# Summing two bit patterns of VectorE's exponential by an accumulating transfer instead of GpSimd, with new order constants

## The chip, the cores and the metric

The kernel runs on one core of a Trainium2 chip. The core's engines run side by side and meet only at semaphores: TensorE (PE in the profile) multiplies matrices into PSUM, ScalarE (ACT) evaluates functions, VectorE (DVE) and GpSimd (POOL) do elementwise work, SyncE (SP) and the queues of the other engines issue DMA transfers. The metric is the device time of one execution in microseconds (us), lower is better.

## The reference

With x of 2048 rows by 448 columns (bf16), the kernel computes `x + s * g`. Both s and g start from the layer-normalised rows xn:

- s is self-attention with 16 heads of 28 columns: `qkv = xn @ wqkv`, scores `q k^T * 28^-0.5`, softmax over the 2048 keys, times v, then `@ wo`.
- g is `silu(gelu(xn @ w1 + b1) @ w2 + b2)` with 1792 hidden columns.

The part that matters here is the softmax: 16 x 2048 x 2048 exponentials, 67 million of them.

## The kernel before, in words

**Tiles.** The scores are made transposed: 128 keys by 512 queries of one head make one score tile, one PSUM bank. Four heads form a head group, four groups of 512 queries a chunk list, so there are 16 blocks (a head group and a query chunk, order `ORD`, line 29) of 64 tiles each (16 key tiles of 4 heads), 1024 tiles in all. A tile goes through three steps: a score matmul (line 1431, K = 28 rows padded to 32, so four heads can share the array by rows), an exponential, and a product with v (the PV matmul, line 1867, four heads side by side in the array's columns) which adds into one PSUM bank `acc`. A column of v holds a constant, so the sum of the exponentials comes out of the same matmul. At the end of a block VectorE copies `acc` away (line 1930), and a chain of small transfers, a reciprocal (line 1949 on GpSimd, or line 1947 on VectorE) and a multiplication (line 1958, GpSimd) normalises it.

**Two ways to an exponential.** Most tiles go to ScalarE, two or three at a time: one ACTIVATE reads two or three PSUM banks (1024 or 1536 columns) and writes bf16 (`fexp`, line 1487). The others are taken in groups of four (the four heads of one key tile) by VectorE. A group's four tiles are read from PSUM, one at a time, by a tensor_scalar that scales and shifts them and writes uint16 (`p_apass`, line 1716): these integers, read as bf16, are a coarse exponential. Two more passes over all four tiles (2048 columns, SBUF to SBUF) add a constant to the integers (`p_expq`, line 1775; constants 40 and 82 of `SH`), which gives three bit patterns of one exponential. Their weighted sum, first pattern times 1 and the other two times `VC` = 0.6875, is the better exponential. The sum is not formed: the PV matmul runs over all three, with v for the first and a copy of v scaled by VC (`vs`, made at line 1800) for the others. So such a group takes 12 PV matmuls instead of 4.

**Summing the two patterns ahead.** The second and third pattern have the same weight, so they may be added beforehand. Then the group needs 8 PV matmuls, and one of its three buffers comes free early. `p_expq` does that on GpSimd where the constants say so (`MG` on, at least `GE` tiles before the block's end, and GpSimd free within `GQ` us): four additions of 128 x 512 (line 1788).

**Buffers.** The patterns live in `unit` buffers of 128 x 2048 bf16, made of space that other tensors no longer use (x_sb, w2, wq, wk, kT, h, xnT, vaug, qsq). There are up to 23 of them, many only late in the kernel. A group begins only when three are free.

**The order.** The instruction order of every engine is fixed when the program is built: a list scheduler in the kernel file (`run`, `start_of`, `put`) walks through time with a duration and a latency for every task and puts the task that can start first. Constants steer it: `BP` has a row for each block of 64 tiles (`p_scores` changes rows), with the pace, the look-ahead and the priorities for that block; `NQ` says how many times per block a VectorE group may be asked for. Which tiles VectorE takes is a result of this walk, so the constants decide how many groups there are. On the chip every engine executes its list in order; a task waits on a semaphore until what it reads is there.

**Other work** fills the gaps between score matmuls: the projections to q, k and v, the two layers of the MLP (lines 1279 and 1348), with one uninterrupted stage where ScalarE evaluates gelu, and at the end the output projection (line 1968). Two thirds down the kernel four output transfers are issued from GpSimd with `accum_op=ALU.add`, onto an output that already holds x (line 1994).

Of the kernel before, what the change touches and what calls it, by code (L numbers as in the profile page):

```python
# [8 lines left out]
ALU = mybir.AluOpType  # L9
ET = mybir.EngineType  # L10

PE, ACT, DVE, POOL, SP = ET.PE, ET.Activation, ET.DVE, ET.Pool, ET.SP
# [16 lines left out]
ORD = [(b // C, b % C) for b in range(11)] + [(3, 0), (3, 1), (3, 2), (2, 3), (3, 3)]  # L29

GM = 584
BPN = ('MG', 'GQ', 'GE', 'EPS', 'PV0', 'PVC', 'MP', 'ND4', 'LU', 'JOINT', 'LQ', 'JMAX', 'DQ', 'URG', 'SLACK', 'UR', 'QLEAD', 'QDIST', 'R3', 'OP')
BP = (
# [17 lines left out]
)  # L51
NQ = (5, 11, 13, 13, 12, 7, 11, 10, 16, 3, 16, 15, 12, 15, 9, 14)
QLEAD, QDIST = 0, 12
JMAX, DQ, LQ, ND4, LU = 2, 3, 2, 3, 3
PV0, PVC, MP = 12, 4, 0.3
SLACK = 0.3
# [4 lines left out]
MG, GQ, GE = 1, 4.0, 12  # L61
GP, MP4, GL = 4.64, 1, 1.2
URG = 12
# [21 lines left out]
    n += k  # L85
SBT = [(f // FT, f % FT) for f in range(F0)]
SEM, OWN = 0.07, 0.03
SWITCH = 0.1
JOINT = 0.05
EPS = 0.1  # L90
# [20 lines left out]


class _Task:
    __slots__ = ("E", "fn", "reads", "writes", "dur", "lat", "rank", "w", "mode", "rows", "port")

    @property
    def prio(self):
# [2 lines left out]
    def __init__(self, E, fn, reads=(), writes=(), dur=0.1, lat=0.05, prio=5, w=1.0, mode="full", rows=(), port=False):  # L120
        self.E, self.fn, self.reads, self.writes = E, fn, list(reads), list(writes)
        self.dur, self.lat, self.rank, self.w = dur, lat, prio, w
        self.mode, self.rows, self.port = mode, set(rows), port
        if E == DVE:
            ov = min(OVERLAP, 0.4 * self.dur)
            self.dur, self.lat = self.dur - ov, self.lat + ov


class _Kernel:
# [74 lines left out]
    def put(self, t, start=None):  # L204
        if start is None:
            start = self.start_of(t)
        self.deps(t.E, t.reads, t.writes)
        if t.E == POOL and t.port:
            self.wait(POOL, self.dve_port)
        sem = self.evsem[t.E]  # L210
        self.evcnt[t.E] += 1
        if t.E == DVE and t.port:
            self.dve_port = (sem, self.evcnt[t.E])
        self.prog[t.E].append(lambda eng, f=t.fn, s=sem: f(eng).then_inc(s, 1))
        h = (sem, self.evcnt[t.E])
        if t.E == PE:
            if t.mode == self.pe_mode == "row" and not (t.rows & self.pe_rows):
                self.pe_rows |= t.rows
            else:
                self.pe_rows = set(t.rows)  # L220
            sw = SWITCH if t.mode != self.pe_mode else 0.0
            self.pe_mode, self.pe_start = t.mode, start
            self.pe_hist.append((start - sw, start + t.dur * t.w))
        if t.port:
            self.port[DVE if t.E == POOL else POOL] = start + t.dur
        self.tE[t.E] = max(self.tE[t.E], start + t.dur)
        self.mark(h, t.reads, t.writes, start + t.dur + t.lat)
        self.log.append((start, t))
        return h
# [158 lines left out]
    def alloc(self):  # L388
# [138 lines left out]
        self.s_qn = [[self.sem("s_qn%d_%d" % (q, c)) for c in range(C)] for q in range(G)]  # L527
        self.s_x0b, self.s_wqk1 = self.sem("s_x0b"), self.sem("s_wqk1")
        self.s_out = [self.sem("s_out%d" % q) for q in range(14)]
        self.s_w = {n: self.sem("s_" + n) for n in ("wqk", "wv", "w1", "w2", "wo", "b")}  # L530

    def schedule(self):
# [911 lines left out]
    def p_scores(self):  # L1444
        K = self
        u = 0
        while K.next_m < MTOT:
            yield ("until", lambda: K.exp_u >= u - 2)
            if K.next_m >= MTOT:
                break  # L1450
            if K.gu is not None and u == K.gu + 1:
                yield ("until", lambda: K.dir_read == ND)
            if K.next_m // 64 != K.blk:
                K.blk = K.next_m // 64
                K.tune(K.blk)
            b0 = 4 * (u % 2)
            n = 2
            ms = []
            while len(ms) < n and K.next_m < MTOT:
                ms.append(K.next_m)  # L1460
                K.step()
            if K.gu is None and ms[-1] >= GM:
                K.gu = u
            at = {m: K.ring[:, b0 + k, :] for k, m in enumerate(ms)}
            toks = [K.b_ring[b0 + k] for k in range(len(ms))]
            K.pend = p = {"task": K.t_score(ms, at, toks, 1), "ms": ms, "at": at, "toks": toks, "rs": [], "b0": b0}
            yield p["task"]
            K.pend = None
            for (m0, u0, m), x in p["rs"]:
                K.spawn(K.p_apass(u0, m0, m - m0, *x), m0)  # L1470
            K.sc_u = u
            u += 1
# [286 lines left out]
    def p_expq(self, m0, u):  # L1759
# [13 lines left out]
        for i in (1, 2):  # L1773
            W, T, bW = *K.pair(us[i], u), K.b_U[us[i]]
            yield _Task(DVE, lambda eng, W=W, T=T, i=i: eng.tensor_scalar(W.bitcast(u16), T.bitcast(u16), float(SH[i]), None, op0=ALU.add),  # L1775
                        bT, bW, 0.69, 0.0, 4, port=True)
        K.ln2e = 0
        if MG and K.next_m < 64 * (m0 // 64 + 1) - GE and K.tE[POOL] < K.now + GQ:
            v, w = us[1:]
            for k in range(0, 4, MP4):  # L1780
# [10 lines left out]
            K.late_ready.append((m0, ((u, 0), (v, 1))))  # L1791
            return
        K.late_ready.append((m0, ((us[0], 0), (us[1], 1), (us[2], 1))))

    def p_vs(self, g):
        K = self
# [275 lines left out]
```

## Time and profile before

| what | value |
|---|---|
| time, median of 3 runs | 419.19 us (419.13 to 419.26) |
| span of the profiled execution, first to last instruction | 417.0 us |
| outside the span, median minus span | 2.2 us |
| granted TensorE clock, mean | 0.999 |
| ScalarE: exponentials of 2 tiles / of 3 tiles | 283 / 74 |
| VectorE: passes from PSUM (line 1716) / integer additions (line 1775) | 236 / 118 |
| GpSimd: additions of two patterns (line 1788) | 52 |
| GpSimd: accumulating output transfers (line 1994) | 4 |

The profile has no time of its own beside its span; the median of the unprofiled runs lies 2.2 us above the span, and this difference is taken as fixed.

How to read it: each page line of a group names the source line, the engine, the operation, what it writes and reads, the shape and the count; behind the first bar the busy time in us and the mean of one in ns; behind the second the engine's idle time just before, and what ended it. Consecutive instructions of ScalarE overlap at their ends, so the distance from start to start, which the timeline gives, says what one costs; its "duration" is longer. The same holds for TensorE's matmuls.

### The profile page before, as it was taken

The page shows a single profiled execution, that of the slowest core. Times are in us where ns is not written, and L with a number is a line of the kernel's source. Part 1 is how long each engine was busy: PE and PEld are TensorE (multiplying, and loading weights), DVE is VectorE, ACT ScalarE, POOL GpSimd, SP SyncE. Part 2 cuts the span into 40 slices and gives each one's busy share as a digit, 9 for nine tenths or more (in the row PEclk, how much of TensorE's full clock was granted, in tenths as well). Part 3 has the DMA queues.
Part 4 walks back from the last instruction along what each step waited for, and adds up shares of the span by engine and source line. Part 5 has one row for each costly group of instructions (what it writes and reads, how often), then busy time and mean ns, then how long its engine had stood idle before and what let it go on. Part 6 is the DMA issues. An engine that isn't in the chain of part 4 may idle for free.

```text
span 417.0 us, 9616 instructions
## 1 busy us (share of the span) xinstructions
PE 400.2 (96%) x3651; PEld 132.6 (32%) x3651; DVE 343.3 (82%) x592; ACT 405.9 (97%) x413; POOL 183.3 (44%) x197
## 2 busy tenths in 40 slices
PE   5899999999999999999999999999999999999995
PEld 4443223332222222222223443222222222333352
DVE  8968899997786899999895115799999888989487
ACT  6999999999999999999999999999999999999995
POOL 7571333237769280204331424408421755680850
PEclk9999999999999999999999999999999999999999
DMA  8801000000001000000240100000010002202061
GB/s 265 271 2 40 3 3 26 14 17 15 26 2 28 0 2 30 2 27 3 54 130 27 25 3 2 2 2 6 21 28 3 10 20 23 50 15 59 4 146 60
DMA packets 15952, 15.29 MB, mean 37 GB/s; under 512 B 7129, under 2 KB 12993, under 8 KB 15874
## 3 DMA queue, kind: packets, MB, share of 16 engines
q1 hardware_dynamic: 15042, 13.07, 11.1%
q0 software_dynamic: 576, 0.92, 1.6%
q8 instruction: 29, 0.48, 0.5%
q10 hardware_dynamic: 288, 0.69, 0.4%
q14 instruction: 17, 0.14, 0.1%
HBM read 12.59 MB, written 2.93 MB: 37 GB/s over the span
## 4 chain that ended last, share of the span: by engine, by line
PE 72%; ACT 15%; DVE 7%; issue 5%; DMA 1%; ACTq 0%; DVEq 0%
PE ring L1431 23%; PE acc L1867 16%; PE ring L1279 9%; ACT P L1487 8%; PE ring L1348 7%; PE misc L1348 4%; PE ring L924 3%; ACT h L1487 3%; PE misc L924 3%; ACT xnT L1487 2%; PE misc L1279 2%; PE misc L1218 2%; PE ring L1218 1%; PE misc L1968 1%; ACT h L1327 1%
## 5 line engine op out<-in xcount | busy, mean ns | idle before, releaser
L1487 ACT ACTIVATE P<-ring 128x1024 bf16<-128x1024 f32 (+1 forms) x237 | 252.9, 1172 | 1.4 <-PE acc L1867 0.5
L1431 PE MATMUL ring<-qT,kT 32*128 32x512 bf16 (+2 forms) x1064 | 142.0, 358 | 6.9 <-ACT P L1487 1.5
L1487 ACT ACTIVATE h<-ring 128x1024 bf16<-128x1024 f32 (+1 forms) x80 | 87.2, 1191 | 0.1
L1431 PEld LDWEIGHTS ring<-qT,kT 32*128 32x128 bf16 x1064 | 38.2, 91 | 143.1 <-ACT P L1487 83.0
L1867 PE MATMUL acc<-P,vaug 128*32 128x512 bf16 (+2 forms) x615 | 54.4, 352 | 0.0
L1279 PE MATMUL ring<-xnT,w 128*128 128x512 bf16 x180 | 48.9, 382 | 0.0
L1949 POOL TENSOR_TENSOR rc<-rs,mone 128x16 f32<-128x16 bf16 x11 | 32.9, 2986 | 30.5 <-DMA rs<-sums 24.2
L1487 ACT ACTIVATE xnT<-ring 128x1024 bf16<-128x1024 f32 (+1 forms) x40 | 45.2, 1157 | 0.3 <-PE ring L1431 0.2
L1958 POOL TENSOR_TENSOR qT<-x_sb,E_sb 128x512 bf16<-128x512 f32 x15 | 17.3, 1156 | 42.9 <-PE acc L1867 22.8
L1348 PE MATMUL ring<-w,h 128*128 128x448 bf16 x140 | 33.6, 355 | 0.4 <-DVE vaug L1716 0.3
L1431 PE MATMUL misc<-qT,kT 32*128 32x512 bf16 (+1 forms) x88 | 32.6, 376 | 0.1
L1716 DVE TENSOR_SCALAR x_sb<-ring 128x512 uint16<-128x512 f32 x43 | 29.1, 686 | 2.6 <-PE ring L1431 2.1
L1173 POOL TENSOR_TENSOR qsq<-qT 128x512 bf16<-128x512 bf16 x12 | 12.5, 1039 | 33.7 <-DVE qT L1167 31.2
L1867 PE MATMUL acc<-h,vaug 128*32 128x512 bf16 x218 | 26.7, 384 | 0.0
L1279 PEld LDWEIGHTS ring<-xnT,w 128*128 128x128 bf16 x180 | 14.7, 97 | 23.8 <-issue 8.3
L1348 PE MATMUL misc<-w,h 128*128 128x448 bf16 x84 | 21.8, 356 | 0.0
L1716 DVE TENSOR_SCALAR h<-ring 128x512 uint16<-128x512 f32 x31 | 20.9, 686 | 0.9 <-PE ring L1431 0.6
L1716 DVE TENSOR_SCALAR x_sb<-misc 128x512 uint16<-128x512 f32 x25 | 17.1, 685 | 4.7 <-PE misc L1431 4.0
L1369 POOL TENSOR_TENSOR h<-w 128x448 bf16<-128x448 bf16 x12 | 12.9, 1072 | 18.1 <-DVE h L1775 16.4
L1867 PEld LDWEIGHTS acc<-P,vaug 128*32 128x32 bf16 x615 | 13.4, 95 | 16.3 <-issue 13.0
L1800 POOL TENSOR_SCALAR vs<-vaug 128x128 bf16<-128x128 bf16 x32 | 9.5, 297 | 20.6 <-DVE w L1775 18.0
L1263 DVE CAST h<-ring 128x512 bf16<-128x512 f32 x21 | 14.4, 685 | 4.4 <-PE ring L1279 4.3
(264 smaller groups left out, 706.4 us busy)
## 6 DMA issues: line engine op xcount, KB each, us to landing
x_sb<-recs SPq DMA_DIRECT2D x60, 64.0 KB, 2.0
w<-in_B_w_dram SPq DMA_DIRECT2D x1, 1568.0 KB, 7.5
w<-in_B_w_dram SPq DMA_DIRECT2D x1, 1344.0 KB, 8.7
x_sb<-in_A_x_dram SPq DMA_DIRECT2D x2, 448.0 KB, 5.0
out_dram<-in_A_x_dram SPq DMA_DIRECT2D x2, 448.0 KB, 10.7
out_dram<-h POOLq DMA_DIRECT2D x4, 224.0 KB, 4.4
out_dram<-h SPq DMA_DIRECT2D x8, 112.0 KB, 1.7
h<-in_A_wqkv_dram SPq DMA_DIRECT2D x3, 168.0 KB, 5.1
```

The lines of the kernel that those rows point to most:

```text
L924: return eng.matmul(bank, w[:, k, g * 128:(g + 1) * 128], K.xnT[:, k, c * 512:(c + 1) * 512], start=(k == 0), stop=(k == KT - 1))
L1218: ins = eng.matmul(bank[:, off:off + nh * DH], K.xnT[:, kt, t * 128:(t + 1) * 128], ap, start=(kt == 0), stop=(kt == KT - 1), skip_group_c ...
L1263: yield _Task(DVE, lambda eng: eng.tensor_copy(dst, bank), [tok], wr, 0.69, 0.0, 2)
L1279: return eng.matmul(bank, K.w1[:, k, ft * 128:(ft + 1) * 128], K.xnT[:, k, c * 512:(c + 1) * 512], start=(k == 0), stop=(k == KT - 1))
L1348: ins = eng.matmul(ps, hv[:, ft, t * 128:(t + 1) * 128], K.w2[:, ft, :], start=(ft == 0), stop=(ft == FT - 1))
L1369: yield _Task(POOL, lambda eng, o=o, t=t: eng.tensor_tensor(o, sg[:, t, :], fb[:, t, :], ALU.mult), [K.b_sig[c % 2], K.b_fsb[c % 2]], [K.b ...
L1431: return eng.matmul(dst, K.kT[32 * j:32 * j + 32, g, t * 128:(t + 1) * 128], K.qT[32 * j:32 * j + 32, g, c * 512 + q0:c * 512 + q0 + nq], ...
L1487: return eng.activation(reg[:, i0:i0 + n, :], K.ring[:, b0:b0 + n, :], ACTF.Exp, scale=SM_SCALE)
L1716: yield _Task(DVE, lambda eng: eng.tensor_scalar(K.part(u, k).bitcast(dt.uint16), K.like(u, bank), SM_SCALE * LOG2E * 128.0, (127.0 - EXP_ ...
L1867: return eng.matmul(K.acc[32 * j:32 * j + 32, q0:q0 + nq], w, ap[:, col:col + nq] if len(ap.shape) == 2 else ap[:, col // 128:(col + nq) / ...
L1949: yield _Task(POOL, lambda eng: eng.tensor_tensor(K.rc[:, :], K.rs[:, :], K.mone[:, 0:1].to_broadcast([128, 16]), ALU.pow), [K.b_srs, K.b_ ...
L1958: yield _Task(POOL, lambda eng: eng.tensor_tensor(dst, K.rb, E, ALU.mult), [K.b_rb, tE], [K.b_onT[g][c]], 1.15, 0.05, 1, port=True)
```

## The change

The third pattern is added to the second by a DMA from SBUF to SBUF that accumulates, issued from GpSimd's queue. Per block a constant `DM` turns it on and `DE` says how many tiles ahead of the block's end it is still used; it isn't used where one of the two buffers is a piece of vaug (three-dimensional). Where the condition does not hold, the old rules for GpSimd's additions apply. The scheduler counts 1.0 us on GpSimd (`DP`) and 4.2 us more until the sum has landed (`DL`). Eight semaphores are used in turn for these transfers. In the program that results 25 groups are summed this way.

All constants of the order are new as well: every row of `BP` (first two columns DM and DE; most rows differ in other columns too, `MG` is now 0 in block 5), and `NQ`. `TW` = 64 replaces a literal 64.

```
-NQ = (5, 11, 13, 13, 12, 7, 11, 10, 16, 3, 16, 15, 12, 15, 9, 14)
+TW = 64
+NQ = (5, 17, 13, 13, 13, 9, 11, 6, 18, 4, 16, 13, 12, 18, 9, 18)
...
+DM, DP, DL = 1, 1.0, 4.2
...
-BPN = ('MG', 'GQ', 'GE', 'EPS', 'PV0', 'PVC', 'MP', 'ND4', 'LU', 'JOINT', 'LQ', 'JMAX', 'DQ', 'URG', 'SLACK', 'UR', 'QLEAD', 'QDIST', 'R3', 'OP')
+BPN = ('DM', 'DE', 'MG', 'GQ', 'GE', 'EPS', 'PV0', 'PVC', 'MP', 'ND4', 'LU', 'JOINT', 'LQ', 'JMAX', 'DQ', 'URG', 'SLACK', 'UR', 'QLEAD', 'QDIST', 'R3', 'OP')
...
-    (0, 4.0, 12, 0.103, 12, 3, 0.124, 4, 16, 0.116, 2, 4, 8, 8, 0.359, 0.922, 18, 20, 0, 5.0),
+    (1, 24, 0, 4.0, 12, 0.103, 12, 3, 0.124, 8, 18, 0.116, 2, 4, 9, 8, 0.359, 0.922, 20, 20, 0, 5.0),
...
@@ put
-        sem = self.evsem[t.E]
-        self.evcnt[t.E] += 1
-        if t.E == DVE and t.port:
-            self.dve_port = (sem, self.evcnt[t.E])
-        self.prog[t.E].append(lambda eng, f=t.fn, s=sem: f(eng).then_inc(s, 1))
-        h = (sem, self.evcnt[t.E])
+        if t.dsem is None:
+            sem = self.evsem[t.E]
+            self.evcnt[t.E] += 1
+            if t.E == DVE and t.port:
+                self.dve_port = (sem, self.evcnt[t.E])
+            self.prog[t.E].append(lambda eng, f=t.fn, s=sem: f(eng).then_inc(s, 1))
+            h = (sem, self.evcnt[t.E])
+        else:
+            sem = t.dsem
+            if id(sem) in self.evcnt:
+                self.wait(t.E, (sem, self.evcnt[id(sem)]))
+            self.evcnt[id(sem)] = self.evcnt.get(id(sem), 0) + 16
+            self.prog[t.E].append(lambda eng, f=t.fn, s=sem: f(eng).then_inc(s, 16))
+            h = (sem, self.evcnt[id(sem)])
...
@@ alloc
+        self.s_add = [self.sem("s_add%d" % q) for q in range(8)]
...
@@ p_expq
         K.ln2e = 0
+        if DM and K.next_m < 64 * (m0 // 64 + 1) - DE and not any(x in (16, 17, 18) for x in us[1:]):
+            yield K.t_add(us[1], us[2])
+            K.free_u.append(us[2])
+            K.n_mg += 1
+            K.late_ready.append((m0, ((u, 0), (us[1], 1))))
+            return
         if MG and K.next_m < 64 * (m0 // 64 + 1) - GE and K.tE[POOL] < K.now + GQ:
...
+    def t_add(self, v, w):
+        K = self
+        dst, src = K.unit[v], K.unit[w]
+        t = _Task(POOL, lambda eng: eng.dma_start(dst, src, accum_op=ALU.add), K.b_U[w] + K.b_U[v], K.b_U[v], DP, DL, 2)
+        t.dsem = K.s_add[K.n_add % len(K.s_add)]
+        K.n_add += 1
+        return t
```

More of the change, by code (lines that the diff above doesn't have):

```diff
@@ L113 @@
 class _Task:
-    __slots__ = ("E", "fn", "reads", "writes", "dur", "lat", "rank", "w", "mode", "rows", "port")
+    __slots__ = ("E", "fn", "reads", "writes", "dur", "lat", "rank", "w", "mode", "rows", "port", "dsem")
     @property
@@ L122, in __init__ @@
         self.dur, self.lat, self.rank, self.w = dur, lat, prio, w
-        self.mode, self.rows, self.port = mode, set(rows), port
+        self.mode, self.rows, self.port, self.dsem = mode, set(rows), port, None
         if E == DVE:
@@ L529, in alloc @@
         self.s_out = [self.sem("s_out%d" % q) for q in range(14)]
+        self.s_add = [self.sem("s_add%d" % q) for q in range(8)]
+        self.n_add = 0
         self.s_w = {n: self.sem("s_" + n) for n in ("wqk", "wv", "w1", "w2", "wo", "b")}
@@ L1452, in p_scores @@
                 yield ("until", lambda: K.dir_read == ND)
-            if K.next_m // 64 != K.blk:
-                K.blk = K.next_m // 64
+            if K.next_m // TW != K.blk:
+                K.blk = K.next_m // TW
                 K.tune(K.blk)
```

32 rows, old and new, of the table BP are left out of this document.

## The prediction

> **What bounds the kernel now.** I read the page first, then the list of instructions by line with shapes kept apart, ScalarE's timeline, the engines' busy time by stretches, the view of the two lines that the change is about (1788 and 1994), and TensorE's chain. Two engines look full in the page.
>
> ```profile
> PE 400.2 (96%) x3651; PEld 132.6 (32%) x3651; DVE 343.3 (82%) x592; ACT 405.9 (97%) x413; POOL 183.3 (44%) x197
> ...
> PE 72%; ACT 15%; DVE 7%; issue 5%; DMA 1%; ACTq 0%; DVEq 0%
> ```
>
> TensorE's share is an upper bound, since its ends are modelled. ScalarE is the one to test: how much of its time is work? Its exponentials by shape (columns: busy us, mean ns, idle before) and a piece of its timeline (start, duration):
>
> ```profile
> L1487 ACT ACTIVATE P<-ring 128x1024 bf16<-128x1024 f32 x186 | 185.5, 1076 | 1.4 <-PE acc L1867 0.5 <-PE ring L1431 0.3
> L1487 ACT ACTIVATE P<-ring 128x1536 bf16<-128x1536 f32 x51 | 76.6, 1523 | 0.0
> ...
> 148.21 3.78 ACT L1487 ACTIVATE P<-ring 128x1024 bf16<-128x1024 f32 x4
> 151.82 2.00 ACT L1487 ACTIVATE h<-ring 128x1024 bf16<-128x1024 f32 x2
> 153.63 1.11 ACT L1487 ACTIVATE P<-ring 128x1024 bf16<-128x1024 f32 x1
> ```
>
> Four exponentials of two tiles take 151.82 - 148.21 = 3.61 us, 0.904 us each from start to start; that is the median of all 283. The 74 of three tiles have a median of 1.330 us. Work: 283 x 0.904 + 74 x 1.330 = 354.2 us. The sum of all distances from start to start behind an exponential is 362.7 us, so ScalarE lost only 8.5 us to waits over the whole kernel. Before the first exponential lie 12.7 us, behind the last some 7 us, and the other 35 us are gelu, tanh and table loads. So 354 of 417 us shrink only if ScalarE gets fewer tiles: 283 x 2 + 74 x 3 = 788 now, and VectorE has 236 (59 groups). TensorE's work can at most give back part of the 8.5 us. The change touches no line of ScalarE; what it is worth is the number of groups that the new order gives to VectorE, less the waits it brings.
>
> **The change part by part.**
>
> *1. GpSimd's additions go.* The 52 of line 1788 are 13 groups at 59.8 us, 1.15 us each. GpSimd is 44% busy, and nothing on TensorE waited for line 1788 directly, so this is worth nothing by itself. But VectorE's integer passes stretch beside GpSimd: 106 of 118 take 0.68 to 0.69 us, twelve 0.75 to 1.37. All 118 take 85.0 us, 118 x 0.684 would be 80.7: 4.3 us of VectorE's time to win at most, 0 at least, since some stand beside other GpSimd lines (1369, 1958).
>
> *2. The transfer comes.* The nearest row is line 1994, also accumulating and issued from GpSimd, 224 KB (columns of the first line: ns min/median/max):
>
> ```profile
> L1994 POOL DMA_DIRECT2D out_dram<-h x4: 871/987/1181, 350.6 to 400.1; - x4
> ...
> DMA to landing us min/median/max: 4.2/4.4/5.0
> ```
>
> Issue: 25 x 1.0 = 25 us of GpSimd instead of the 59.8, while the engine has 234 us free. Its queue is in order: behind a transfer that waits for VectorE's second pass stand the normalising steps (lines 1949, 1958), but the additions of line 1788 waited there for the same pass (13.2 us on h, 11.7 on xnT and so on), so this is no new wait. SP's queue isn't passed. Landing: in the first of the four, 1.67 us pass from the issue's start to the first packet, 2.2 us to the last packet, 0.35 us to the semaphore. The new transfer has 512 KB in rows of 4096 instead of 1792 bytes. Low end: rows cost no more, 4.2 us. High end: packets scale with bytes, 1.67 + 2.2 x 4096/1792 + 0.35 = 7.0 us. The order reckons with 1.0 + 4.2 = 5.2; its other constants fit the rows (0.69 for line 1716's 0.686, 1.16 for line 1788's 1.15). I take 5.7, half-way, so 0.5 us late.
>
> Who suffers if a sum lands late? TensorE, whose PV matmuls stand in order before the next score matmuls. How soon they come shows in the 13 groups of before: from the end of the last addition to the first matmul that reads it there are 1.7 to 6.7 us, mean 4.2. An example (start, duration):
>
> ```profile
> 324.08 4.48 POOL L1788 TENSOR_TENSOR h<-h,kT 128x512 bf16<-128x512 bf16 x4 [2.96 <-PE ring L1348]
> ...
> 334.54 0.39 PE L1867 MATMUL acc<-h,vs 128*32 128x512 bf16 x4
> ```
>
> The sum is there at 328.56 and used at 334.54. With such gaps 0.5 us late costs nothing; at 7.0, 1.8 us late, one of the 13 gaps would fall short by 0.1 us. I book +0.4 us for shorter gaps in the new order (range 0 to 3).
>
> *3. PV matmuls go.* 25 sums instead of 13 are 12 x 4 matmuls less, if no group that GpSimd summed is left beside them. What four cost is in the chain (start, us, what):
>
> ```profile
> 65.89 1.19 PE acc L1867 x20
> 72.33 0.76 PE acc L1867 x12
> 102.33 0.98 PE acc L1867 x16
> ```
>
> 0.22 us for each four, so 12 x 0.22 = 2.6 us of TensorE. It lies under ScalarE's row of exponentials and counts as nothing; were ScalarE not full there, it would be worth up to 2.6.
>
> *4. The order constants.* A further group takes two exponentials from ScalarE: 2 x 0.904 = -1.81 us. On VectorE it costs 4 x 0.686 + 2 x 0.684 = 4.11 us. On TensorE it removes two score steps (about 0.22 us each, an estimate from the same four-wide matmuls) and adds one or two fours of PV: about nothing. Requests don't limit: eight key tiles per block may be taken, and the sum of min(NQ, 8) is 119 before and after, against 59 groups. VectorE's time and buffers do. VectorE's time by stretches (us, then busy of PE, PEld, DVE, ACT, POOL):
>
> ```profile
> 60.00:100.00 40.00, 39.49 (x364) 13.11 (x362) 36.07 (x62) 40.00 (x39) 14.83 (x18) 1.00 0.07 18
> 100.00:140.00 40.00, 39.37 (x315) 10.97 (x317) 29.99 (x48) 40.00 (x40) 30.73 (x31) 1.00 0.07 15
> 140.00:180.00 40.00, 38.87 (x333) 10.10 (x325) 38.84 (x63) 39.99 (x43) 12.44 (x8) 1.00 0.05 14
> ```
>
> From 100 to 140 us, where GpSimd is busiest (30.7 of 40 us, with additions), VectorE works 30.0, its neighbours 36.1 and 38.8. Filled to 36.1, this stretch gives 6.1 us; with the 4.3 us of part 1 that is 10.4 us, 2.5 groups. Low end: no group more (the free time is held by buffers, or the constants gain nothing). High end: NQ's sum rises from 182 to 195, 7%, and 7% of 59 is 4 groups. I take 2: -3.6 us.
>
> *Sum.* 417.0 - 3.6 + 0.4 = 413.8 us of span, and 2.2 us around it: 416.0. From part 4's and part 2's ends this case runs from 417.0 - 7.2 + 0 + 2.2 = 412.0 to 417.0 - 1.8 + 3 + 2.2 = 420.4; as "faster" it ends at 418.3.
>
> **The rivals.** *Late transfers (slower).* The landing, not the work, decides. Against the 13 gaps, a landing at L us leaves a shortfall whenever L - 5.2 exceeds the gap, and of each some 0.5 us is covered, since ScalarE has one exponential (0.9 us) in hand while TensorE stands. L = 8.5 (3.3 late): six of 13 fall short, by 5.3 us together, of which 2.7 are covered; scaled to 25, 2.6 x 25/13 = 5.0 us lost, more than the 3.6 won. So from about 8.4 us on it is slower. At 9 the same count gives 10.2, so 425.8. [...] Against: issues of line 1994 spread only from 0.87 to 1.18 us.
>
> [...]
>
> *No more groups.* The transfers only replace additions, buffers hold VectorE back as before. Then ScalarE keeps 788 tiles: 418.6 (part of the 8.5 us of waits won) to 420.0. For it: freeing the third buffer 5.2 us later is no sooner than GpSimd's 4.6. Against: that comes for 25 groups, not 13.
>
> *The new order waits more (slower).* Every constant changed, and waits of 8.5 us are hard to keep; 4 us more with the same groups is 423. Against: the order's durations fit this trace.
>
> **How the numbers follow.** Within 0.2% (0.84 us) a measurement can't tell this kernel from no change. More groups, transfers in time: 0.61 (412.0 to 418.3, all faster). No more groups: 0.16, of which 0.08 same, 0.03 faster and 0.05 slower. Late transfers: 0.14, 420 to 428. More waits: 0.09, 420 to 425. So faster 0.64, same 0.08, slower 0.28. Time of the likeliest: 416.0. The range keeps out about a tenth on each side: 411.5 to 423.5; low is 2.5 groups' worth under 416.0.
>
> **What would show it.** Right: fewer than 788 tiles on line 1487 (each group less is two exponentials), more than 236 passes of line 1716, 25 DMA issues from `t_add` at about 1.0 us landing in 4.2 to 7.0, ScalarE's waits still near 8.5 us, and integer passes nearly all at 0.684. Wrong: TensorE waiting at line 1867 for a DMA; landings beyond 8 us; GpSimd's issues stretched beside the integer passes; or the same 788 tiles.

## The result, and the profile after

| | before | changed |
|---|---|---|
| time, median (13 executions each) | 419.19 us (418.92 to 420.04) | 423.29 us (420.73 to 425.10) |
| ratio | | 1.0088, 95% interval 1.0068 to 1.0108 |
| span of the profiled execution | 417.0 us | 421.5 us |
| ScalarE: exponentials of 2 tiles / of 3 tiles | 283 / 74 (788 tiles) | 311 / 54 (784 tiles) |
| VectorE: groups of four tiles | 59 | 60 |
| ScalarE: work of the exponentials | 354.3 us | 353.0 us |
| ScalarE: waits between exponentials | 8.5 us | 14.0 us |

The changed kernel is 0.9% slower, and the interval lies wholly above 1. An execution takes about 1.8 us more than its own span (423.29 and 421.5 for the profiled one); the 2.2 us named for the kernel before set the median of several executions against the span of one. One correction to the description of the change: 25 groups are summed ahead, but 20 by a transfer and five still by GpSimd (20 additions at line 1806). The lines of the file move by 12 to 26: the exponential is now line 1499, the score matmul 1443, the PV matmul 1893, VectorE's integer pass 1787, the accumulating transfer 1816.

The page of the changed kernel, the lines on busy time, granted clock by 40 slices, GpSimd's DMA queue and the chain that ended last:

```profile
PE 400.2 (95%) x3583; PEld 131.8 (31%) x3611; DVE 343.1 (81%) x598; ACT 406.3 (96%) x421; POOL 167.3 (40%) x185
PEclk9999999999996999999999999999999999999999
q0 software_dynamic: 3456, 11.40, 14.8%
PE 72%; ACT 11%; DVE 8%; issue 5%; DMA 3%; SPq 1%; DVEq 0%; ACTq 0%
```

Three things differ from before. The clock row has a 6 in slice 13, near 127 us. GpSimd's queue carries 11.4 MB, where it carried 0.92 (576 packets, 1.6%). The chain has 3% DMA and a new share of SP's queue, where it had 1% DMA. ScalarE's exponentials by shape, to be read against the two lines shown of before:

```profile
L1499 ACT ACTIVATE P<-ring 128x1024 bf16<-128x1024 f32 x206 | 201.4, 1076 | 3.0 <-PE ring L1443 1.6 <-PE misc L1443 0.4 <-PE acc L1893 0.3
L1499 ACT ACTIVATE P<-ring 128x1536 bf16<-128x1536 f32 x39 | 57.9, 1491 | 0.5 <-PE ring L1443 0.5
```

The idle time before the first group went from 1.4 to 3.0 us, and what ended it is mostly a score matmul. ScalarE does less work and waits more.

**Two kinds of execution.** The 13 executions fall into groups by their mean granted clock. Four at 1.0 took 420.73 to 421.56 us; nine at 0.986 to 0.996 took 422.20 to 425.10. The profiled one is of the second kind. A later profile of the same kernel (e12 below) is of the first, and it makes the account simple. In us, by the starts of ScalarE's exponentials:

| part of the span | before | changed, clock 1.0 | changed, with the dip |
|---|---|---|---|
| ahead of the first exponential | 12.7 | 13.1 | 12.9 |
| exponentials | 354.3 | 353.0 | 353.0 |
| waits between them | 8.5 | 11.2 | 14.0 |
| gelu, tanh, table loads | 33.5 | 33.1 | 33.1 |
| from the last exponential's start to the end | 8.1 | 8.5 | 8.5 |
| span | 417.0 | 418.8 | 421.5 |

So there are two questions: what makes 1.8 us at full clock, and where the dip comes from.

**The dip.** Busy time by stretches of the changed kernel (us; PE, PEld, DVE, ACT, POOL busy, then granted clock, DMA share, GB/s):

```profile
118.00:122.00 4.00, 3.55 (x40) 1.01 (x38) 3.81 (x7) 4.00 (x5) 3.31 (x10) 1.00 0.06 10
122.00:127.00 5.00, 4.57 (x32) 1.46 (x32) 5.00 (x9) 5.00 (x7) 2.93 (x1) 0.98 0.57 107
127.00:134.00 7.00, 6.53 (x44) 1.29 (x46) 4.59 (x9) 5.58 (x6) 0.00 (x0) 0.53 0.12 40
```

The same stretches of the kernel before:

```profile
118.00:122.00 4.00, 4.00 (x35) 1.10 (x27) 3.55 (x6) 4.00 (x5) 2.62 (x4) 1.00 0.02 1
122.00:127.00 5.00, 4.92 (x40) 1.53 (x41) 4.68 (x8) 5.00 (x5) 3.73 (x2) 1.00 0.00 0
127.00:134.00 7.00, 6.93 (x54) 2.00 (x56) 4.04 (x7) 7.00 (x9) 6.88 (x8) 1.00 0.19 41
```

From 126.8 us on the clock is 0.5 for 6.8 us. In the 9 us ahead of it TensorE was busy 8.1 us, in the kernel before 8.9. (The changed kernel's profile without the dip shows the same 8.1, so the dip doesn't come each time with it.) What thinned the stage shows in TensorE's groups between 118 and 127 us. The matmuls there that use the whole array, before:

```profile
L1279 PE MATMUL ring<-xnT,w 128*128 128x512 bf16 x8 | 2.4, 385 | 0.0
L924 PE MATMUL misc<-xnT,wq 128*128 128x512 bf16 x4 | 1.4, 384 | 0.0
L924 PE MATMUL ring<-xnT,wk 128*128 128x512 bf16 x4 | 1.0, 382 | 0.0
L1279 PE MATMUL misc<-xnT,w 128*128 128x512 bf16 x2 | 0.6, 380 | 0.0
```

and changed:

```profile
L1095 PE MATMUL acc<-ident,zero 128*128 128x128 bf16 x6 | 0.7, 223 | 0.0
L1291 PE MATMUL misc<-xnT,w 128*128 128x512 bf16 x2 | 0.6, 384 | 0.0
```

Of 18 matmuls of the q and k projections and of the MLP's first layer two are left; the new order does the others elsewhere. PV matmuls are 32 in both, score matmuls 23 before and 32 changed. Line 1095 multiplies zeros: the scheduler of both kernels puts three such matmuls where its own count of TensorE's work is low (`pe_low`). The two sets that it put here, at 121.6 and 125.2 us, did not keep the clock up: it was 0.5 from 126.8 us on.

In the dip ScalarE works 5.58 of 7 us where it worked all 7. The timeline of TensorE shows what a matmul then takes (start, duration):

```profile
120.98 0.39 PE L1443 MATMUL ring<-qT,kT 32*128 32x512 bf16 x2
...
127.18 0.61 PE L1893 MATMUL acc<-P,vaug 128*32 128x512 bf16 x1
...
131.16 0.61 PE L1443 MATMUL ring<-qT,kT 32*128 32x512 bf16 x3
```

0.39 us becomes 0.61. Three of ScalarE's waits follow, 0.99 us at 127.3, 0.61 at 130.3 and 0.56 at 133.3; before has none over 0.3 us there.

**The transfers.** Their view (issues and landing):

```profile
who waited for it (us, times):
  DVE x_sb L1787: 0.4, 1
  PEld acc L1893: 0.4, 1
...
DMA to landing us min/median/max: 4.5/4.7/6.2
```

They land as bounded, and nobody waits more than 0.4 us for one. But between 188 and 199 us others wait (timeline; start, duration; in brackets the engine's idle time before):

```profile
187.85 1.03 POOL L1816 DMA_DIRECT2D h<-w  x1 [3.27 <-DVE w L1787]
...
189.05 0.86 POOL L1816 DMA_DIRECT2D kT<-h  x1 [0.18 <-issue]
...
189.38 0.49 SPq L1968 DMA_DIRECT2D sums<-E_sb  x1
...
192.78 0.86 POOL L1816 DMA_DIRECT2D h<-x_sb  x1 [2.86 <-DVE x_sb L1787]
...
194.14 0.35 SPq L1970 DMA_DIRECT2D rs<-sums  x1
194.53 3.01 SPq L1217 DMA_DIRECT2D qT<-qst  x4
...
198.37 0.39 PE L1443 MATMUL ring<-qT,kT 32*128 32x512 bf16 x2 [0.76 <-DMA qT<-qst]
...
198.80 1.02 ACT L1499 ACTIVATE h<-ring 128x1024 bf16<-128x1024 f32 x1 [0.55 <-PE ring L1443]
```

SP issues `sums<-E_sb`, a 4 KB transfer, at 189.38, and the next link of that chain, `rs<-sums`, waits for it: 4.76 us from one issue to the other, where it is 1.6 for most blocks. (One step is longer still, at 207 us, but there 6.99 us in the kernel before too.) Two 512 KB transfers had been issued just before. SP's list is in order, so four q-norm transfers (`qT<-qst`, rows of the next head group's queries) stand behind `rs<-sums` and start late too; TensorE waits for them, and ScalarE for TensorE. In the kernel before, the same four went out at 159.3 us, ahead of the sums at 169: the new order put them behind. For the sums themselves only GpSimd waits (5.22 us, line 1975).

### The profile page after: what moved, and what is told of

The parts are those of the page before. It is cut to its first block, busy times and chain, and to the rows that moved or that the text cites. A ratio compares the mean times of both kernels' runs of the same rounds, so it can differ in the third digit from the quotient of the medians.

```text
span 421.5 us, 9542 instructions
## 1 busy us (share of the span) xinstructions
PE 400.2 (95%) x3583; PEld 131.8 (31%) x3611; DVE 343.1 (81%) x598; ACT 406.3 (96%) x421; POOL 167.3 (40%) x185
## 4 chain that ended last, share of the span: by engine, by line
PE 72%; ACT 11%; DVE 8%; issue 5%; DMA 3%; SPq 1%; DVEq 0%; ACTq 0%
PE ring L1443 23%; PE acc L1893 18%; PE ring L1291 9%; ACT P L1499 7%; PE ring L1360 7%; PE ring L936 4%; PE misc L1360 3%; ACT h L1499 3%; PE misc L1291 2%; PE misc L936 2%; PE ring L1230 1%; PE misc L1994 1%; DMA h<-in_A_wqkv_dram 1%; DMA qT<-qst 1%; DVE w L1728 1%
## 5 line engine op out<-in xcount | busy, mean ns | idle before, releaser
L1443 PE MATMUL ring<-qT,kT 32*128 32x512 bf16 (+2 forms) x1043 | 146.5, 360 | 8.0 <-ACT P L1499 1.0
L1291 PE MATMUL ring<-xnT,w 128*128 128x512 bf16 x162 | 43.9, 384 | 0.8 <-issue 0.8
L1360 PE MATMUL ring<-w,h 128*128 128x448 bf16 x168 | 41.3, 356 | 0.0
L1499 ACT ACTIVATE xnT<-ring 128x1024 bf16<-128x1024 f32 (+1 forms) x38 | 40.2, 1124 | 0.3 <-PE ring L1443 0.2
L1443 PE MATMUL misc<-qT,kT 32*128 32x512 bf16 (+1 forms) x109 | 40.0, 375 | 0.1
L1728 DVE TENSOR_SCALAR x_sb<-ring 128x512 uint16<-128x512 f32 x31 | 21.1, 687 | 4.2 <-PE ring L1443 4.1
L1728 DVE TENSOR_SCALAR vaug<-ring 128x512 uint16<-128x512 f32 x26 | 17.3, 687 | 2.4 <-PE ring L1443 1.5
L1360 PEld LDWEIGHTS ring<-w,h 128*128 128x128 bf16 x168 | 12.1, 97 | 17.9 <-issue 11.2
L1816 POOL DMA_DIRECT2D h<-w x5 | 4.7, 930 | 30.3 <-DVE w L1787 27.4
L1339 ACT ACTIVATE h<-h 128x1536 bf16<-128x1536 bf16 (+1 forms) x12 | 16.5, 1373 | 0.0
```

What stands on the lines that cost most here:

```text
L1291: return eng.matmul(bank, K.w1[:, k, ft * 128:(ft + 1) * 128], K.xnT[:, k, c * 512:(c + 1) * 512], start=(k == 0), stop=(k == KT - 1))
L1339: yield _Task(ACT, lambda eng, dst=dst, src=src: eng.activation(dst, src, ACTF.Gelu_apprx_tanh), rd, wr, 0.4267 * n + (0.1 if pc else 0.06 ...
L1360: ins = eng.matmul(ps, hv[:, ft, t * 128:(t + 1) * 128], K.w2[:, ft, :], start=(ft == 0), stop=(ft == FT - 1))
L1443: return eng.matmul(dst, K.kT[32 * j:32 * j + 32, g, t * 128:(t + 1) * 128], K.qT[32 * j:32 * j + 32, g, c * 512 + q0:c * 512 + q0 + nq], ...
L1499: return eng.activation(reg[:, i0:i0 + n, :], K.ring[:, b0:b0 + n, :], ACTF.Exp, scale=SM_SCALE)
L1728: yield _Task(DVE, lambda eng: eng.tensor_scalar(K.part(u, k).bitcast(dt.uint16), K.like(u, bank), SM_SCALE * LOG2E * 128.0, (127.0 - EXP_ ...
```

## The experiments

The theory, formed from this: (1) the clock dip comes from TensorE's thin stage at 118 to 127 us and costs 2 to 2.5 us whenever it comes; (2) the transfers cost 1 to 1.6 us, through small transfers that they slow down; (3) the order, with its one more group and more waits, is no gain. The rivals: the dip is the chance of one chip; the cost is the transfers' waits on GpSimd's queue, or their issue beside VectorE's passes.

### e1 and e2: idle matmuls against the dip

```
+        if t.E == PE and t.mode == "row" and 112 <= start < 128 and self.pv_started and not self.copying:
+            self.filler()          # e2: 16 <= start < 400
...
+            for _ in range(3):
+                eng.matmul(K.acc[:, 0:128], K.zero[:, :], K.ident[:, :], start=False, stop=True, ...)
```

> The changed kernel in its own order, with three idle matmuls (zero weights, 128 columns) put ahead of each score step that the order places between 112 and 128 us. Clock theory: the changed order leaves TensorE thin around 118 to 127 us, the granted clock halves there for some 7 us in most executions, and that is 2 to 4 us of the loss. Then the dip at 127 us is gone from the trace, the mean granted clock is 1.00 in nearly all executions and the median falls from 423.3 to 420.7 to 421.6 us, what the undisturbed executions of the changed kernel take. Rival, the dip only follows a delay that comes from elsewhere (the transfers): clock 0.99 and 423 us as before.

> The same idle matmuls ahead of every score step from 16 to 400 us, so that no stage of the changed order is thin. Clock theory: clock 1.00 in all executions, 420.7 to 421.6 us with a spread under 1 us; if the dips of other executions lie in other stages, this one is steadier than the kernel with one stage filled. Rival, TensorE has no room for them: 340 steps x 0.16 us are 54 us more work, part of it lands on the path and the time rises above 424 us.

Measured: e1 426.88 us (426.22 to 427.81; ratio to before 1.018, 1.0158 to 1.0201), e2 495.77 us (ratio 1.182, 1.180 to 1.184), both at a clock of 0.995 to 1.0. The dip is gone from both profiles (one execution of e1's five still stood at 0.995), but both are slower than the changed kernel, where I had expected 420.7 to 421.6. In e1 ScalarE's waits from 119.9 to 132.1 us alone sum to 6 us. In e2 there are 1110 more matmuls, 370 fillers, and the span is 75 us longer than the changed kernel's at full clock (493.9 against 418.8), so 0.20 us for each filler of 3 x 128 columns. The timeline of e2 (start, duration) shows that none of it is hidden:

```profile
150.88 0.39 PE L1454 MATMUL ring<-qT,kT 32*128 32x512 bf16 x2
151.20 0.34 PE L248 MATMUL acc<-ident,zero 128*128 128x128 bf16 x3
151.47 0.38 PE L1454 MATMUL ring<-qT,kT 32*128 32x512 bf16 x1
```

One score step to the next takes 0.59 us, 0.32 to the filler and 0.27 behind it. The score matmuls use 32 rows of the array and the filler all 128; what of the 0.20 us is the filler's own matmuls and what the change of shape on both sides of it, no run here separates. As a cure of the dip the filler is useless; as a test it confounds the dip with its own price. Hence e5.

### e3: the transfers left out

```
-        t = _Task(POOL, lambda eng: eng.dma_start(dst, src, accum_op=ALU.add), ...)
-        t.dsem = K.s_add[K.n_add % len(K.s_add)]
+        t = _Task(POOL, lambda eng: eng.memset(one, 0.0), ...)
```

> The changed kernel in its own order, but the 20 accumulating transfers are left out: GpSimd clears one column of a spare tile in their place, so the third pattern is missing in the result of those 20 groups. Contention theory: the transfers hold up the small transfers of the softmax sums and of the q norms on SP's queue, TensorE and VectorE wait for these at 198 us and near 398 us, 0.8 us each. Then executions with a clock of 1.00 take 419.3 to 419.8 us instead of 420.7 to 421.6, and SP's step from the sums to their next transfer is 1.6 us in every block. If the clock dip also comes from the transfers, the median is 419.5; if it comes from the order, most executions stay near 422. Rival, the transfers are hidden and the order alone is slower: 423.3 us, 421 at full clock.

Measured: 422.21 us (418.98 to 423.18, 12 executions), ratio 1.0051 (1.0027 to 1.0075). Four executions at clock 1.0 took 418.98 to 419.74, median 419.5; eight at 0.988 to 0.992 took 421.58 to 423.18. So the dip comes without any transfer, in two of three executions: it belongs to the order. At full clock 419.5 stands against 421.07, the median of the first four of the changed kernel: the transfers cost some 1.6 us. The same 419.5 against 418.84, what before takes in the median at a clock of 0.999 to 1.0 on this chip, says that the order alone is 0.7 us slower, by four executions of which one (418.98) lies among those of before. SP's step from `sums<-E_sb` to `rs<-sums` at 190 us is 1.60 us here, against 4.76 with the transfers. ScalarE's waits at 197 and 399 us of the changed kernel are gone; those at 364, 376, 381 and 385 us (0.39 to 0.71 us) stay, so they are the order's.

### e5: the score matmuls of the thin stage issued twice

```
+        twice = 114 <= K.now < 128
-            for f in fl:
+            for f in (fl + fl if twice else fl):
```

> The changed kernel in its own order, where each score matmul that the order places between 114 and 128 us is issued twice in a row (same operands, same result), so TensorE is busier there without a change of the array's tiling; filler of another tiling cost 3 us by itself. Clock theory: the dip of the granted clock near 127 us does not come, executions have a mean clock of 0.995 or more, and the median is 420.7 to 421.8 us with a spread near 1 us. Rival, the dip has nothing to do with how busy TensorE is in this stage: clock 0.986 to 0.992 in two thirds of the executions and a median of 423.

Measured: 421.75 us (421.35 to 422.31), ratio 1.0059 (1.0045 to 1.0074), clock 0.999 to 1.0 in all six. The same stretches as above:

```profile
118.00:122.00 4.00, 4.00 (x54) 0.91 (x46) 3.39 (x6) 3.60 (x5) 2.72 (x9) 1.00 0.22 40
122.00:127.00 5.00, 5.00 (x53) 1.76 (x50) 4.79 (x9) 4.62 (x5) 3.96 (x2) 1.00 0.57 106
127.00:134.00 7.00, 6.72 (x70) 1.95 (x70) 6.15 (x11) 6.61 (x8) 0.00 (x0) 1.00 0.14 40
```

TensorE is busy for all of the 9 us up to 127 us, and the clock stays at 1.00. The four kernels with this edit (e5, e8, e9, e10) had a clock of 0.998 or more in 21 of 21 executions; the three without it (the changed kernel, e3, e11) had it under 0.997 in 24 of 40. So with more work on TensorE in that stage the dip didn't come; whether the share of busy time or the shift of the stage that the doubling brings is what counts isn't parted by it. The kernel before isn't free of such losses: 7 of its 63 executions beside these runs stood at 0.995 and took 420.35 to 420.95 us; no profile shows where. The doubling costs something itself (new waits of 0.58, 0.49 and 0.52 us at 120, 123 and 129 us), which eats most of what it saves.

The half clock lasted 6.8 us in the changed kernel's profile and 10.2 us in e3's, and the changed kernel meets it in some executions of the same instructions (11 of 20) and not in others. What sets its length, why only some executions meet it, and how thin a stage must be, no run here shows.

### e4, e6 and e7: the kernel before, with idle transfers

24 transfers of 448 KB (22 of them accumulating) from GpSimd's queue into memory that nobody reads, added to the kernel before with waits as in the change (e4); the same waits with no transfer (e6); the transfers without the waits (e7).

```
+        if K.next_m < 64 * (m0 // 64 + 1) - 24:
+            K.idle_add(us[2])
...
+        K.deps(POOL, K.b_U[w] + [K.b_wo], [])        # e7: K.deps(POOL, [K.b_wo], [])
...
+        K.prog[POOL].append(lambda eng: eng.dma_start(K.scr.ap()[i], ..., accum_op=ALU.add).then_inc(...))
                                                       # e6: eng.memset(one column) instead
```

> The kernel before in its own order, with 24 transfers of 448 KB added on GpSimd's queue behind the last integer pass of a group that lies over 24 tiles ahead of its block's end, 22 of them accumulating, from a constant tile into a scratch tensor in DRAM that nobody reads. Nothing waits for them but the end. Contention theory: they delay the small transfers of the same core; depending on what then waits, 0.5 to 3 us more, 419.7 to 422. Rival, transfers beside this kernel are harmless: 419.2 us within 0.2%, and the loss of the changed kernel is its order's alone.

> The kernel before with the 24 waits on GpSimd's queue of the run with added transfers, but a clear of one column instead of each transfer. It splits that run's loss of 4.0 us: if the transfers' share of the DMA engines causes it, this kernel takes 419.2 us within 0.2%; if GpSimd's queue, held until VectorE's pass is done, causes it, this takes 423.

> The kernel before with the 24 transfers at the same places of GpSimd's list but without the wait for VectorE's pass, so each is issued as soon as GpSimd gets to it. If transfers on the shared DMA engines and GpSimd's 1 us for each issue cause the loss, it stays at 2 us or more, 421 to 424; if it is the wait in GpSimd's queue, the time is 419.2 to 420.

Measured: e4 423.24 us, ratio 1.0091 (1.0071 to 1.0111); e6 419.27, ratio 1.0003 (0.9990 to 1.0015); e7 420.39, ratio 1.0029 (1.0018 to 1.0041). The waits alone cost nothing, as the prediction had said. The transfers alone cost 1.0 us, both together 4.0, more than the sum. (e4 lies above the 422 that I had expected at most, e7 between its two expectations.) In e4 VectorE's 118 integer passes take 10.7 us more than 118 x 0.684, in before 4.3, in e7 5.7. VectorE's timeline in e4 (start, duration):

```profile
333.19 1.54 DVE L1780 TENSOR_SCALAR h<-x_sb 128x2048 uint16<-128x2048 uint16 x1
334.65 0.68 DVE L1721 TENSOR_SCALAR xnT<-ring 128x512 uint16<-128x512 f32 x1
335.25 1.20 DVE L1780 TENSOR_SCALAR qsq<-x_sb 128x2048 uint16<-128x2048 uint16 x1
```

and of GpSimd and TensorE at the same time:

```profile
333.14 1.04 POOL L1376 TENSOR_TENSOR h<-h,w 128x448 bf16<-128x448 bf16 x1
...
334.87 1.03 POOL L1374 TENSOR_TENSOR h<-w 128x448 bf16<-128x448 bf16 x1 [0.69 <-DVE h L1780]
...
337.13 0.39 PE L1436 MATMUL ring<-qT,kT 32*128 32x512 bf16 x2 [0.71 <-DVE w L1359]
```

The two passes run beside GpSimd's steps and take 1.54 and 1.20 us, where in the kernel before they took 0.68 and 1.13, and TensorE waits 0.71 us for VectorE behind them. In the kernel before, GpSimd's step of two inputs ended at 330.66 us, ahead of the first pass at 330.83; in e4 the two start together (333.14 and 333.19). Of the 21 stretched passes only two stand beside a DMA issue. So shifted steps of GpSimd may cost more than the transfer that shifts them; that this makes up the 3 us between e7 and e4 isn't shown. In the changed kernel this didn't happen (6.0 us of stretch against 4.3), so e4 tells of a danger, not of the cause here.

### e8 and e9: all transfers left out, and four of them

Both on top of e5, so that the dip is away. e8 leaves out all 20 as e3 did; e9 only the three at 187 to 193 us and the one at 390 us.

```
+        if K.n_add in (8, 9, 10, 19):
+            t = _Task(POOL, lambda eng: eng.memset(one, 0.0), ...)
+        else:
+            t = _Task(POOL, lambda eng: eng.dma_start(dst, src, accum_op=ALU.add), ...)
```

> Both cuts in the changed kernel's own order: no accumulating transfers (the third pattern is missing in 20 groups) and the score matmuls between 114 and 128 us issued twice. What is left is the new order at full clock. If the loss is the transfers' 1.6 us, the dip's 1.5 to 3 us and an order that is no better, it takes 419.8 to 420.5 us: the 421.75 us of the run with doubled scores less 1.6, in a spread under 1.5 us. Rival, the dip and the transfers hide each other: it stays at 421 or more.

> The changed kernel with the score matmuls between 114 and 128 us issued twice, and with only four of the 20 transfers left out (a clear of one column instead, the third pattern missing in these four groups): the three issued between 187 and 193 us, whose neighbours are the sums and the q norms of that block, and the last one at 390 us, beside the sums of the last full block. Contention with these small transfers: the gain is 1.3 to 1.6 us, 420.1 to 420.5 us, as with all 20 left out. Rival, all 20 cost a little each: a fifth of 1.6 us, 421.4.

Measured: e8 421.21 us (420.71 to 421.46), ratio 1.0051; e9 421.27 us (420.76 to 421.33), ratio 1.0051. Both expectations were too low: the sum of the two savings isn't reached, since the doubling keeps its own price of about 1.7 us (421.2 against e3's 419.5). What they do say: four transfers left out give the same as all 20. Against e5, the start times of e9's exponentials show one jump, 0.75 us at 198.5. The wait at the end of the kernel isn't there in e5 either, so these two couldn't test it; e11 does.

### e10: the q-norm transfers ahead in SP's list

```
+        n0 = len(K.prog[SP])                     # ahead of the loop that issues them
...
+        if g == 2 and K.at_rs is not None:       # the four qT<-qst of this head group
+            q = K.prog[SP][n0:]
+            del K.prog[SP][n0:]
+            K.prog[SP][K.at_rs:K.at_rs] = q      # ahead of rs<-sums
...
+            K.at_rs = len(K.prog[SP])            # between sums<-E_sb and rs<-sums
```

> The kernel with doubled score matmuls at 114 to 128 us (no clock dip there), all 20 transfers kept; the one change against it: the four q-norm transfers that stood behind rs<-sums in SP's list at 194 us are issued ahead of it. Theory, small transfers that are slowed by the 512 KB ones hold SP's in-order queue, and the q-norm transfers behind them hold TensorE: the wait of 0.7 us at 197 to 199 us goes, 421.75 - 0.75 = 421.0 us at clock 1.0. Rival, the q-norm transfers themselves are slow beside the 512 KB ones wherever they stand: the wait remains, 421.75 us.

Measured: 421.04 us (420.74 to 421.18), ratio 1.0046 (1.0033 to 1.0059). Against before at full clock on the same chip (418.84) that is 2.2 us, for e5 on its chip (418.84) 2.9: 0.7 less, where the theory had 0.75. Timeline:

```profile
188.53 0.49 SPq L1975 DMA_DIRECT2D sums<-E_sb  x1
189.86 3.46 SPq L1218 DMA_DIRECT2D qT<-qst  x4
...
193.37 0.44 SPq L1978 DMA_DIRECT2D rs<-sums  x1
198.44 3.37 POOL L1983 TENSOR_TENSOR rc<-rs,mone 128x16 f32<-128x16 bf16 x1 [5.65 <-DMA rs<-sums]
```

The small chain is as slow as ever (4.84 us from `sums<-E_sb` to `rs<-sums`, and 5.07 more until line 1983 starts), with all 20 transfers in place. But the q-norm transfers no longer stand behind it, and ScalarE's wait at 197 us is gone. So the cost at this place was SP's order behind a slowed transfer: it takes both, the 512 KB transfers (without them, in e11, the step is 1.60 us) and the place in the list.

### e11 and e12: four transfers left out alone, and the changed kernel again

e11 is e9 without the doubling; e12 is the changed kernel as it is.

> The changed kernel with only four of the 20 transfers left out (those at 187 to 193 us and the one at 390 us; the third pattern is missing in four groups). Score matmuls are not doubled, so the clock dip at 127 us stays in two of three executions. Theory, these four carry all that the transfers cost: executions at clock 1.0 take 419.5 us (as with all 20 left out), the others 421.6 to 423.2. Rival, only the wait at 198 us is theirs and the rest is spread: executions at clock 1.0 take 420.3 us.

> The changed kernel once more, beside the other two on the same chip. Theory: executions at clock 1.0 take 420.7 to 421.6 us, those with the dip at 127 us 422.2 to 425.1, median near 423. With the dip put down to chance it should again come in more than half of the executions; if it came from the chip of the first runs it would be missing here, and the median would be 421.

Measured: e12 420.68 us (420.54 to 424.23, seven executions), ratio 1.0059 (1.0036 to 1.0083). Five had a clock of 0.998 or more and took 420.54 to 420.77; two had the dip (0.992 and 0.987) and took 423.06 and 424.23. I had expected the dip in more than half; it came in two of seven, together with the first executions in 11 of 20. So the median depends on how many executions meet it, and it isn't a matter of one chip. e11: 421.63 us (419.28 to 423.15), three executions at 0.998 or more of 419.28 to 419.73, five with the dip of 421.62 to 423.15.

On this one chip and at full clock: changed 420.68, without the four transfers 419.48, before 418.84. The four cost 1.2 us, and with them go ScalarE's waits of 0.69 us at 194.5 and 0.64 us at 396.6 of e12. The second place, in e12:

```profile
386.94 0.88 POOL L1816 DMA_DIRECT2D x_sb<-x_sb  x1 [3.94 <-DVE x_sb L1787]
...
388.07 3.30 SPq L1965 DMA_DIRECT2D rs<-E_sb  x4
...
393.77 0.25 DVE L1973 RECIPROCAL rc<-rs 128x16 f32<-128x16 bf16 x1 [1.63 <-DMA rs<-E_sb]
...
396.16 0.40 PE L1443 MATMUL ring<-qT,kT 32*128 32x128 bf16 x12 [0.38 <-DVE h L2011]
```

and in e11, where the transfer at 388 us is a memset:

```profile
388.48 0.10 POOL L1819 MEMSET scr<- 128x1 f32 x1 [3.69 <-DVE x_sb L1788]
...
389.86 3.75 SPq L1970 DMA_DIRECT2D rs<-E_sb  x4
...
394.78 0.25 DVE L1978 RECIPROCAL rc<-rs 128x16 f32<-128x16 bf16 x1 [0.86 <-DMA rs<-E_sb]
```

From the first issue of the four 1 KB transfers to VectorE's reciprocal it is 5.70 us beside the big transfer and 4.92 without. VectorE, in order, stands at the reciprocal 1.63 us instead of 0.86; line 2011 behind it comes late, TensorE waits for it (0.38), ScalarE for TensorE (0.64).

## Why the prediction was wrong, step by step

**What bounds the kernel: right on the work, one-sided on the waits.** In both kernels the span is ScalarE's work, its waits and its two ends, and the ends and the work outside the exponentials moved by at most 0.4 us each. TensorE was said to be able to give back part of the 8.5 us of waits at most. The waits grew instead: 11.2 us at full clock, 14.0 with the dip.

**Part 1, GpSimd's additions: right on its worth, off in size.** They went from 52 to 20, not to 0. VectorE's stretch beside GpSimd, of which up to 4.3 us was to be won, is 6.0 us now; nothing was won, and that belonged to the gain of part 4.

**Part 2, the transfers: the landing right, the bystanders missed.** Landing was bounded by 4.2 and 7.0 us and is 4.5 to 6.2, median 4.7, where the sum took 5.7; issues took 0.86 to 1.40 us; nobody waited more than 0.4 us. The waits on GpSimd's queue cost nothing (e6, ratio 1.0003). The step that failed in this part is "SP's queue isn't passed". The transfers don't stand in SP's list, but they move 512 KB each beside SP's 1 to 4 KB transfers and stretch a step to 4.76 us that takes 1.60 at this place without them (e3, e11). The price was 1.2 us in e11 (1.6 by e3), where the term allowed +0.4 for PV matmuls alone, and four of the 20 transfers carry it.

**Issues beside integer passes,** whose stretch the prediction named as a sign against it, decided nothing. In the profile of before line 1994's issue at 354.95 us took 1.18 us, and the pass at 355.31 took 0.75. Ten issues of the changed kernel's profile stand beside an integer pass and take 0.86 to 1.40 us; one pass there is stretched, by 0.5 us, and the eleven others take 0.68 to 0.70 us. e7 shows the worst: issues up to 1.63 us and five passes stretched by 2.6 us together. All six stretched passes also stand beside an elementwise step of GpSimd, so that an issue alone does this to a pass isn't shown.

**Part 3, fewer PV matmuls: nothing, as booked, and a little smaller.** By its weight loads the PV line has 1540 matmuls where it had 1580: 40 less. The 48 of the forecast are gone, and the one group more adds 8. (The page's counts, 3651 and 3583 matmuls, differ by 68, but the changed profile lacks 28 matmul records; it has 3611 weight loads.) The dip isn't theirs: the thin stage has 32 PV matmuls in both kernels.

**The clock: a term put at nothing without a reason.** The sum carries over the clock of before, 0.999. In 11 of 20 executions of the new order it falls (means of 0.986 to 0.996); in the profiled one it halves for 6.8 us at the end of the stage at 118 to 127 us. The cost is 2.2 to 2.4 us, by the median of each kind (423.4 against 421.07 in the first runs, 421.7 against 419.5 in e11). The new order took 16 of 18 matmuls of projections and MLP out of this stage. Which of its constants did that, and whether these 16 put back would keep the clock, wasn't tried; doubled score matmuls did (e5).

**Part 4, the constants: the step with the largest error at full clock.** Two groups more were booked, -3.6 us; one came, -1.8, and 60 tiles moved from triples to pairs: 20 x 1.330 = 26.6 us as triples, 30 x 0.904 = 27.1 as pairs, +0.5. So -1.3. VectorE's free time between 100 and 140 us bounded the groups only from above, and the high end used the requests' sum of 195, although the same paragraph finds that requests don't limit (119 by min(NQ, 8), before and after). And the order's own waits, which were assumed to stay near 8.5 us, grew: e3 at full clock, with the gain and without any transfer, is 0.7 us slower than before.

**The sum.** The forecast was a gain, 416.0 us; the result is a loss, 423.29. Against before's 418.84 at full clock: order +0.64 (e11, which still has 16 transfers), the four transfers +1.20 (e12), so 420.68. In the first runs 1.6 for the transfers: 421.07. The dip brings their median to 423.29, and before's own small losses of clock bring its median to 419.19. An estimate of the way from 416.0, from these figures: a gain of 1.3 us instead of 3.6, +2.3; the order's other time, 0.64 + 1.3, +1.9; the transfers, 1.2 instead of 0.4, +0.8; the dip, 423.29 - 420.68, +2.6; and 1.8 us around the span instead of 2.2, -0.4. Together 423.2.

**The rivals.** "Late transfers" didn't happen: the landings were 4.5 to 6.2 us, where it needed about 8.4. "No more groups" was nearly so. "The new order waits more", with 423 the nearest in time, was right that waits grow and by luck near in size: of the 5.5 us more, 2.8 come with the dip (14.0 - 11.2), 1.3 with the four transfers (0.69 + 0.64), and the rest is the order's own, such as the four waits at 364 to 385 us. What it had against it, that the order's durations fit the trace, was true of durations alone; the load of the DMA engines and a clock under 1.0 don't stand in them.

No version beat the kernel before. An estimate: the changed kernel with e10's edit alone would be 420.68 - 0.75 = 419.9 at full clock, still above 418.84, and the dip would stay.

## What to carry to other kernels

A large transfer that meets its own deadline can still cost, at a small transfer that is under way beside it (here a step of 1.60 us took 4.76, and four of 20 transfers cost 1.2 us): list those, what stands behind them in their queue, and who waits for that. Moving work of TensorE out of a stage was not free here (8.1 of 9 us busy instead of 8.9, and a clock of 0.986 to 0.996 in 11 of 20 executions, at 2.2 to 2.4 us): look at the granted clock of each execution, not of one, when the times of a kernel fall into two groups. When one edit comes with a new order, leave out the edit's work and keep the order: that one run parted the two here.

## What the runs showed of the hardware that I had not expected

- The same instructions ran at a granted clock of 1.0 in some executions and with 6.8 to 10.2 us at half clock in others; the matmuls then took 0.61 instead of 0.39 us, and the kernel 2.2 to 2.4 us more.
- Fillers of the full array between score matmuls that use 32 rows cost 0.20 us each, with nothing hidden: 75 us for 370 of them.
- Two sets of three zero matmuls in a stage of 9 us with TensorE 8.1 us busy did not keep the clock from halving behind it.
- 4 KB and 1 KB transfers beside transfers of 512 KB: a step of 1.6 us took 4.8 us (4 KB), and one of 4.9 us took 5.7 (four of 1 KB).
- 24 idle transfers cost the kernel before 1.0 us when free to go and 4.0 us when each waited for its group, though the waits alone cost nothing. The stretched passes beside GpSimd's shifted steps are seen; that they make up the whole 3 us isn't shown.
